# A gated mix of a state-space layer and a feed-forward layer: three parameter loads placed behind the w1 loads, and their four small products later on TensorE

## The chip, the cores and the metric

One Trainium2 chip, one core of it. The metric is the time of one execution on the device in microseconds (us). TensorE (PE) multiplies into PSUM, which has 8 banks here; VectorE (DVE), ScalarE (ACT) and GpSimd (POOL) compute on SBUF; SyncE (SP) only issues transfers (DMAs). All engines run their own instructions in order and wait for each other by semaphores.

## The reference, cut to what matters

```python
x = A_x                                        # [1, 2048, 448], bf16
g = sigmoid((x * gate_w).sum(-1, keepdims=True))
Lam = Lambda_re + 1j * Lambda_im               # 448 channels
dt = exp(log_dt)
Lam_bar = exp(dt * Lam)
B_bar = ((Lam_bar - 1.0) / Lam)[:, None] * (B_re + 1j * B_im)
Bu = einsum("bld,pd->blp", x + 0j, B_bar)
h_t = Lam_bar * h_{t-1} + Bu_t                 # over 2048 tokens
a = 2.0 * einsum("blp,dp->bld", h, C_re + 1j * C_im).real + x * Dskip
b = silu(x @ w1) @ w2                          # w1 [448, 1792], w2 [1792, 448]
out = g * a + (1 - g) * b
```

## The kernel before, in words

The 2048 tokens are taken in four chunks of 512. For each chunk TensorE computes x times w1 (14 blocks of 128 columns, called F tiles) and x times B (7 blocks, B tiles; real and imaginary rows of 448 channels are packed in 7 slots). ScalarE applies silu while it copies the F tiles from PSUM to `aT` (L634); the B tiles go to `UG` (by VectorE at L640 for the first chunk, by ScalarE at L642 after). The complex recurrence is turned into a real one: `UG` is rotated by the angles of each token (tables `COS` and `SIN`, products L704 on VectorE), a scan runs along the tokens with a real factor `rc` (L736), and the result is rotated back into `H`. The readout multiplies `H` by prepared rows of C (`CP`, L795), the second feed-forward product multiplies `aT` by w2 (L774), ScalarE scales that to `fe` (L780), GpSimd's DMA adds it to what the gate made of x (L782), and VectorE joins the two and SP stores (L798, L801).

**Tables and parameters.** `parameters()` (L529 to L589) needs the three vectors log_dt, Lambda_re and Lambda_im, each loaded as one row of 448 values into `prm`. VectorE copies 64 of their columns behind the others (L538), four products on TensorE with a 3x3 identity turn the rows into columns (L536), VectorE copies them out (`pc`, L540), GpSimd takes e to the power of log_dt (L543), and VectorE makes the angle `ph` of each channel (L544) and its fraction of a turn (L524, L527). From `ph` VectorE and ScalarE build `SIN` and `COS` (L555 to L566), the factors of the recurrence and, at last, the scales of C.

**Loads.** w1 is loaded in column groups, `w1cuts = [0, 256, 512, 1024, 1792]`. A group's rows come in two loads, rows 0 to 383 and rows 320 to 447 (w1 has 448 rows, and the second load repeats 64 of them); group 0 is split further. `load()` (L387, DMA issue at L390) gives each load the next number as its priority, so SP's queue follows the order of the calls at L401 to L441: half of x, half of group 0, the three parameters, groups 1 and 2 (two loads each), B (four loads), group 3, the gate and skip vectors, the second chunk of x, w2, C, the rest of x. The other half of x and of group 0 goes on ScalarE's queue.

**TensorE's order** is written out by hand. `x_products` (L647) takes tiles in pairs; each pair accumulates in two banks, in two halves: `half(k, 0)` has 8 matmuls and `half(k, 1)` 6, after which the pair is evicted. The order is half(0, 0), then for each k half(k+1, 0) and half(k, 1). A dictionary `fill` puts other work between: key -1 right behind half(0, 0), key k behind step k, key (k, 0) behind the first of step k's two halves, which is half(k+1, 0) for most. The first two pairs of F tiles need w1's groups 0 and 1, the third and fourth group 2.

**The other engines' order** comes from a planner (`Plan.order`, L104): it simulates the engines with a cost for each operation and takes, at each point, the ready operation of the lowest priority number. What it finds is fixed: each engine then runs that list in order. So a change in one place can reorder VectorE, ScalarE and GpSimd everywhere.

Of the kernel before, what the change touches and what calls it, by code (L numbers as in the profile page):

```python
# [276 lines left out]
def bass_gated_mix__ssm_conv_s5__dense_activation_silu__prompt_kernel(nc, A_x, A_Lambda_re, A_Lambda_im, A_B_re, A_B_im, A_C_re, A_C_im,  # L277
               A_log_dt, A_Dskip, B_x, B_w1, B_w2, gate_w, out):
    with ExitStack() as ctx:
# [3 lines left out]
        def sb(name, shape, dtype):  # L283
            return E(nc.sbuf_tensor(name, list(shape), dtype))
# [38 lines left out]
        prm = sb("prm", [3, 512], BF16)  # L323
# [30 lines left out]
        def sem():  # L354
            _s[0] += 1
            return E(nc.semaphore(name=f"d{_s[0]}"))
# [30 lines left out]
        def load(q, dst, src, name, nbytes, prio=None, after=()):  # L387
            nl[0] += 1
            prio = nl[0] if prio is None else prio
            P.add(q, lambda e: e.dma_start(dst, src), list(after), name.split(), 0.6 if q == "pool" else 0.5, prio, sem(), nbytes, tag="ld " + name)  # L390
# [3 lines left out]
        def load_w1(q, k, a, b):  # L394

            cols = slice(w1cuts[k], w1cuts[k + 1])
            src = B_w1[320:448, cols] if a == 3 else B_w1[128 * a:128 * b, cols].rearrange("(b p) f -> p b f", p=128)
            load(q, w1s[:, 3, cols] if a == 3 else w1s[:, a:b, cols], src, " ".join(f"w1_{k}_{i}" for i in range(a, b)),
                 256 * (b - a) * (cols.stop - cols.start))
# [3 lines left out]
        load_w1("sp", 0, 0, 2)  # L403
        load_w1("act", 0, 2, 3)
        load_w1("act", 0, 3, 4)
        for k, v in enumerate((A_log_dt, A_Lambda_re, A_Lambda_im)):
            load("sp", prm[k:k + 1, 0:448], v.rearrange("(o n) -> o n", o=1), f"prm{k}", 896)
        for k in range(1, len(w1cuts) - 2):
            load_w1("sp", k, 0, 3)
            load_w1("sp", k, 3, 4)  # L410
        Bnat = H[3][:, :, 0:D_MOD]
        load("sp", Bnat[:, 0:3, :], A_B_re[0:384, :].rearrange("(b p) d -> p b d", p=128), "H3_0 H3_1 H3_2", 384 * 896)
        load("sp", Bnat[0:64, 3, :], A_B_re[384:448, :], "H3_3", 64 * 896)
# [84 lines left out]
        def x_transposes(tc, who):  # L498

            tk = Ps(2)  # L500

            def mm(pe):
                for q in range(4):
                    for b in range(4):
                        o = (q * 4 + b) * 64
                        for h in range(2):
                            p = slice(64 * h, 64 * h + 64)
                            r = pe.transpose(bk(tk, h).bitcast(BF16)[:, o:o + 64],  # L508
                                             xnat[p, 4 * tc + b, XCOL[q]:XCOL[q] + 128], ident[p, p])
                return r  # L510
            PE(mm, [f"xn{tc}", "ident"], [tk], 16 * 0.035, f"xT{tc}")
            for h in range(2):
                src = lambda h=h: bk(tk, h).bitcast(BF16).rearrange("p (q b n) -> p q b n", q=4, b=4)
                dst = xT[:, :, tc * CH:(tc + 1) * CH].rearrange("p q (b h n) -> p q b h n", h=2, n=64)[:, :, :, h, :]
                if who[h] == "d":
                    DVE(lambda e, src=src, dst=dst: e.tensor_copy(dst, src()), [tk], [f"xT{tc}_{h}"], 0.69, 2.2, "xTe")
                else:
                    ACT(lambda e, src=src, dst=dst: e.activation(dst, src(), AF.Copy), [tk], [f"xT{tc}_{h}"], act_cost(1024), 2.2, "xTe")
# [74 lines left out]
        def b_transposes(s0, s1, who):  # L593

            tk = Ps(2)
            n = s1 - s0

            def mm(pe):
                for i in range(4):
                    for q in range(n):  # L600
                        o = (i * n + q) * 64
                        for h in range(2):
                            p = slice(64 * h, 64 * h + 64)
                            r = pe.transpose(bk(tk, h).bitcast(BF16)[:, o:o + 64], Bnat[p, s0 + q, XCOL[i]:XCOL[i] + 128], ident[p, p])  # L604
                return r
            PE(mm, [f"H3_{s}" for s in range(s0, s1)] + ["H3_3i"] * (s0 <= 3 < s1) + ["ident"], [tk], n * 4 * 0.0285, "BT")
            for h in range(2):
                src = lambda h=h: bk(tk, h).bitcast(BF16)[:, 0:256 * n].rearrange("p (i s c) -> p i s c", i=4, s=n)
                dst = BT[:, :, :].rearrange("p i (s h c) -> p i s h c", h=2, c=64)[:, :, s0:s1, h, :]
                names = [f"BT{s}_{h}" for s in range(s0, s1)]  # L610
                if who[h] == "d":
                    DVE(lambda e, src=src, dst=dst: e.tensor_copy(dst, src()), [tk], names, 0.15 + n * 0.136, 2, "BTe")
                else:
                    ACT(lambda e, src=src, dst=dst: e.activation(dst, src(), AF.Copy), [tk], names, act_cost(256 * n), 2, "BTe")
# [82 lines left out]
        def F(tc, a=0, b=NFB):  # L697
            return [("F", tc, k) for k in range(a, b)]

        def B(tc):  # L700
            return [("B", tc, k) for k in ((3, 0, 4, 1, 5, 2, 6) if tc else (0, 1, 2, 3, 4, 5, 6))]
# [131 lines left out]
        def gates(tc):  # L833
            xnn = ["xn00", "xn01"] if tc == 0 else [f"xn{tc}"]
            b4 = slice(4 * tc, 4 * tc + 4)
            tt(xg[:, :, :], xnat[:, b4, :], gwb[:, None, :].to_broadcast([128, 4, D_MOD]), ALU.mult,
               xnn + ["gwb"] + (["Gf0"] if tc else []), ["xg"], 1792, 19, "xg")
            tt(xnat[:, b4, :], xnat[:, b4, :], dkb[:, None, :].to_broadcast([128, 4, D_MOD]), ALU.mult,
               xnn + ["dkb"] + (["Gf0"] if tc else []), [f"xd{tc}"] + xnn, 1792, 19, "xd")
            for b in range(4):  # L840
                tb = 4 * tc + b
                ACT(lambda e, tb=tb, b=b: e.activation(junk[:, :], xg[:, b, :], AF.Copy, accum_out=zl[:, tb:tb + 1]),  # L842
                    ["xg"], ["junk", f"zl{tc}"], act_cost(448, 1), 8, "z")
            ACT(lambda e: e.activation(th[:, b4], zl[:, b4], AF.Tanh, scale=0.5), [f"zl{tc}", "tbl"], [f"th{tc}"], 0.25, 8)
            ACT(lambda e: e.activation(g1[:, b4], th[:, b4], AF.Copy, scale=-0.5, bias=0.5), [f"th{tc}"], [f"g1_{tc}"], 0.2, 3, "g")
            ACT(lambda e: e.activation(g[:, b4], th[:, b4], AF.Copy, scale=0.5, bias=0.5), [f"th{tc}"], [f"g_{tc}"], 0.2, 3, "g")
            for b in range(4):
                tb = 4 * tc + b
                ACT(lambda e, tb=tb: e.activation(Tb[:, tb, :], xnat[:, tb, :], AF.Copy, scale=g[:, tb:tb + 1]),  # L849
                    [f"xd{tc}", f"g_{tc}"], [f"Tb{tb}"], act_cost(448, 1), 8, "xd*g")  # L850

        def xt(tc, who):
            return [lambda: x_transposes(tc, who)]
# [7 lines left out]
        def C(*tbs):  # L861
            return [lambda tb=tb: readout(tb) for tb in tbs]

        turn_b = [lambda: b_transposes(0, 2, "da"), lambda: b_transposes(2, 4, "da"), lambda: b_transposes(4, 7, "da")]
        NH = 8
        K = NH // 2
        x_products(F(0, 0, NH) + B(0) + F(0, NH) + B(1),
                   {-1: [parameters], (K - 2, 0): turn_b[:1], K - 2: turn_b[1:2], K - 1: turn_b[2:], 7: xt(1, "da") + [lambda: lanes(0)]}, [K - 2])
        gates(0)
        gates(1)  # L870
        lanes(1)
# [47 lines left out]
```

## Time and profile before

| | |
|---|---|
| median of 3 runs | 142.11 us (142.05 to 142.25) |
| the profiled execution | 141.99 us |
| its span, first to last instruction | 140.2 us |
| granted TensorE clock | 1.000 |
| TensorE busy | 135.7 us, 97% of the span |
| VectorE busy | 122.3 us, 87% |
| ScalarE busy | 89.7 us, 64% |
| GpSimd busy | 38.9 us, 28% |

The busy rows tell how full an engine is, not what sets the end. That is read from the chain that ended last, which follows the work back from the last instruction to whatever released it. Two of its kinds of piece are no computing: "SPq" is SP issuing transfers, one after the other, and "DMA" is a transfer that something waited for. In the timelines each row has a start, a duration, the engine, the line and the tile written; `x4` behind it means four instructions in a row; a bracket at the end gives the idle time of that engine just before, and what ended it. In the table by stretches each engine has its busy time and its count of instructions, and the last three columns are the granted clock, the DMA engines' busy share and their GB/s.

### The profile page before, as it was taken

The page shows a single profiled execution, that of the slowest core. Times are in us where ns is not written, and L with a number is a line of the kernel's source. Part 1 is how long each engine was busy: PE and PEld are TensorE (multiplying, and loading weights), DVE is VectorE, ACT ScalarE, POOL GpSimd, SP SyncE. Part 2 cuts the span into 40 slices and gives each one's busy share as a digit, 9 for nine tenths or more (in the row PEclk, how much of TensorE's full clock was granted, in tenths as well). Part 3 has the DMA queues.
Part 4 walks back from the last instruction along what each step waited for, and adds up shares of the span by engine and source line. Part 5 has one row for each costly group of instructions (what it writes and reads, how often), then busy time and mean ns, then how long its engine had stood idle before and what let it go on. Part 6 is the DMA issues. An engine that isn't in the chain of part 4 may idle for free.

```text
span 140.2 us, 2999 instructions
## 1 busy us (share of the span) xinstructions
PE 135.7 (97%) x1201; PEld 67.7 (48%) x1201; DVE 122.3 (87%) x179; ACT 89.7 (64%) x157; POOL 38.9 (28%) x72
## 2 busy tenths in 40 slices
PE   7979999999999999999999999999999999999992
PEld 2536554455544544455554544444455555555561
DVE  0486999999999999999999999999999999992053
ACT  3239978999999996713961886799930298011300
POOL 7340030202436500139550003732000223122220
PEclk9999999999999999999999999999999999999999
DMA  4899999610466730109985000946002304323332
GB/s 159 248 356 263 370 297 209 194 42 0 72 108 107 115 40 0 37 0 137 148 145 136 0 5 0 151 92 101 0 0 101 65 0 70 72 91 54 47 91 73
DMA packets 17956, 14.71 MB, mean 105 GB/s; under 512 B 2835, under 2 KB 17814, under 8 KB 17942
## 3 DMA queue, kind: packets, MB, share of 16 engines
q0 software_dynamic: 6064, 5.51, 24.8%
q1 hardware_dynamic: 11318, 8.65, 21.0%
q10 hardware_dynamic: 560, 0.36, 0.8%
q8 instruction: 9, 0.15, 0.4%
q14 instruction: 5, 0.04, 0.1%
HBM read 7.17 MB, written 1.84 MB: 64 GB/s over the span
## 4 chain that ended last, share of the span: by engine, by line
PE 92%; DMA 3%; SPq 2%; issue 0%; DVE 0%
PE ps L663 44%; PE ps L774 30%; PE ps L795 15%; DMA w1s<-in_B_w_dram 3%; SPq L390 2%; PE ps L508 1%; PE ps L814 1%; PE ps L604 1%; DVE ot L798 0%
## 5 line engine op out<-in xcount | busy, mean ns | idle before, releaser
L663 PE MATMUL ps<-xT,w1s 64*128 64x512 bf16 x392 | 48.2, 376 | 0.9 <-DMA w1s<-in_B_w_dram 0.9
L774 PE MATMUL ps<-w2s,aT 128*128 128x448 bf16 x224 | 43.2, 353 | 0.0
L634 ACT ACTIVATE aT<-ps 128x1024 bf16<-128x1024 f32 (+1 forms) x30 | 28.5, 966 | 11.2 <-PE ps L663 11.1
L774 PEld LDWEIGHTS ps<-w2s,aT 128*128 128x128 bf16 x224 | 21.7, 98 | 20.4 <-issue 0.4
L663 PEld LDWEIGHTS ps<-xT,w1s 64*128 64x128 bf16 x392 | 19.8, 94 | 22.8 <-DMA w1s<-in_B_w_dram 1.4
L663 PE MATMUL ps<-xT,BT 64*128 64x512 bf16 x196 | 25.8, 376 | 0.0
L782 POOL DMA_DIRECT2D xnat<-fe x16 | 14.2, 890 | 41.5 <-ACT fe L780 35.7
L780 ACT ACTIVATE fe<-ps,g 128x448 bf16<-128x448 f32 x16 | 10.1, 631 | 19.9 <-PE ps L774 19.9
L390 POOL DMA_DIRECT2D UG<-Gf x27 | 14.8, 555 | 26.1 <-DVE Gf L736 25.8
L798 DVE SCALAR_TENSOR_TENSOR ot<-ps,g,xnat 128x448 bf16<-128x448 f32 (+2 forms) x18 | 10.8, 626 | 8.0 <-issue 6.6
L736 DVE TENSOR_TENSOR_SCAN Gf<-rc,gin,H 128x512 f32<-128x512 f32 x14 | 17.0, 1268 | 0.0
L795 PE MATMUL ps<-CP,H 128*128 128x448 bf16 (+2 forms) x98 | 16.4, 326 | 0.0
L663 PEld LDWEIGHTS ps<-xT,BT 64*128 64x128 bf16 x196 | 11.1, 94 | 10.9 <-issue 0.2
L704 DVE TENSOR_TENSOR H<-UG,COS 128x3584 bf16<-128x3584 bf16 (+4 forms) x10 | 12.7, 1270 | 0.0
L795 PEld LDWEIGHTS ps<-CP,H 128*128 128x128 bf16 x98 | 8.9, 98 | 7.5 <-DVE PO L704 0.4
L642 ACT ACTIVATE UG<-ps 128x1024 bf16<-128x1024 f32 (+1 forms) x12 | 10.9, 919 | 1.3 <-PE ps L663 1.3
L390 POOL DMA_DIRECT2D UG<-UG x8 | 4.5, 564 | 24.3 <-ACT UG L642 13.6
L842 ACT ACTIVATE junk<-xg 128x448 bf16<-128x448 bf16 x16 | 9.3, 579 | 3.0 <-DVE xg L704 2.9
L849 ACT ACTIVATE xnat<-xnat,g 128x448 bf16<-128x448 bf16 x16 | 9.9, 659 | 0.3
L704 DVE TENSOR_TENSOR PI<-UG,SIN 128x512 bf16<-128x512 bf16 (+2 forms) x13 | 9.2, 728 | 0.0
L704 DVE TENSOR_TENSOR PO<-UG,SIN 128x1536 bf16<-128x1536 bf16 (+1 forms) x8 | 8.7, 1085 | 0.3 <-DMA UG<-Gf 0.2
L736 DVE TENSOR_TENSOR_SCAN Gf<-rc,gin,H2C 128x512 f32<-128x512 f32 x7 | 8.6, 1270 | 0.0
(102 smaller groups left out, 126.5 us busy)
## 6 DMA issues: line engine op xcount, KB each, us to landing
UG<-Gf POOLq DMA_DIRECT2D x21, 128.0 KB, 2.3
xnat<-fe POOLq DMA_DIRECT2D x16, 112.0 KB, 2.6
out_dram<-ot SPq DMA_DIRECT2D x15, 112.0 KB, 1.7
w2s<-in_B_w_dram SPq DMA_DIRECT2D x1, 1568.0 KB, 11.5
xnat<-in_A_x_dram SPq DMA_DIRECT2D x3, 448.0 KB, 6.6
w1s<-in_B_w_dram SPq DMA_DIRECT2D x1, 576.0 KB, 5.4
UG<-UG POOLq DMA_DIRECT2D x8, 64.0 KB, 2.0
H2C<-in_A_C_re_dram SPq DMA_DIRECT2D x2, 196.0 KB
```

The costliest lines, as they stand in the source:

```text
L390: P.add(q, lambda e: e.dma_start(dst, src), list(after), name.split(), 0.6 if q == "pool" else 0.5, prio, sem(), nbytes, tag="ld " + name)
L634: ACT(lambda e, src=src, dst=dst: e.activation(dst, src(), AF.Silu), [tk, "tbl"], [f"aT{tc % 2}_{m}" for m in names], act_cost(512 * n), 2 ...
L642: ACT(lambda e, src=src, dst=dst: e.activation(dst, src(), AF.Copy), [tk], [f"{un}{m}" for m in names], act_cost(512 * n), 5, "U")
L663: r = pe.matmul(bk(toks[k], b), weights(tile, p0, p0 + 64, i), xT[p0:p0 + 64, i, tc * CH:(tc + 1) * CH], start=(h == 0 and n == 0), stop=( ...
L704: DVE(lambda e: e.tensor_tensor(o, a, b, op), r, w, dve_cost(n, 2), prio, tag)
L736: DVE(lambda e, s=s, b=b, init=init: e.tensor_tensor_scan(Gf[:, s, :], rc[:, b:b + 1].to_broadcast([128, CH]), A[:, s, :], init, ALU.mult, ...
L774: r = pe.matmul(bk(tk)[:, 0:D_MOD], aT[tc % 2][:, fb, o:o + 128], w2s[:, fb, :], start=(fb == 0), stop=(fb == NFB - 1))
L780: ACT(lambda e: e.activation(f[:, :], bk(tk)[:, 0:D_MOD], AF.Copy, scale=g1[:, tb:tb + 1]), [tk, f"g1_{tc}"], [fn], act_cost(448, 1), 7, "fe")
L782: P.add("pool", lambda e: e.dma_start(Tb[:, tb, :], f[:, :], accum_op=ALU.add), [fn, f"Tb{tb}"], [f"Tb{tb}"], 0.94, 2, sem(), 115000, tag= ...
L795: r = pe.matmul(bk(tk)[:, 0:b - a], H[tc][:, s, o:o + 128], CP[:, s, a:b], start=(s == 0), stop=(s == NSLOT - 1))
L798: DVE(lambda e, tk=tk, a=a, b=b: e.scalar_tensor_tensor(ot[tb % NOT][:, a:b], bk(tk)[:, 0:b - a], g[:, tb:tb + 1], Tb[:, tb, a:b], ALU.mul ...
L849: ACT(lambda e, tb=tb: e.activation(Tb[:, tb, :], xnat[:, tb, :], AF.Copy, scale=g[:, tb:tb + 1]), [f"xd{tc}", f"g_{tc}"], [f"Tb{tb}"], ac ...
```

## The change

```diff
         load_w1("sp", 0, 0, 2)
         load_w1("act", 0, 2, 3)
         load_w1("act", 0, 3, 4)
-        for k, v in enumerate((A_log_dt, A_Lambda_re, A_Lambda_im)):
-            load("sp", prm[k:k + 1, 0:448], v.rearrange("(o n) -> o n", o=1), f"prm{k}", 896)
         for k in range(1, len(w1cuts) - 2):
             load_w1("sp", k, 0, 3)
             load_w1("sp", k, 3, 4)
+        for k, v in enumerate((A_log_dt, A_Lambda_re, A_Lambda_im)):
+            load("sp", prm[k:k + 1, 0:448], v.rearrange("(o n) -> o n", o=1), f"prm{k}", 896)
         Bnat = H[3][:, :, 0:D_MOD]
...
         x_products(F(0, 0, NH) + B(0) + F(0, NH) + B(1),
-                   {-1: [parameters], (K - 2, 0): turn_b[:1], K - 2: turn_b[1:2], K - 1: turn_b[2:], 7: xt(1, "da") + [lambda: lanes(0)]}, [K - 2])
+                   {(1, 0): [parameters], (K - 2, 0): turn_b[:1], K - 2: turn_b[1:2], K - 1: turn_b[2:], 7: xt(1, "da") + [lambda: lanes(0)]}, [K - 2])
```

On SP's queue the three parameter loads move behind the four loads of w1's groups 1 and 2 and ahead of B's. On TensorE the four small products move from behind half(0, 0) to behind half(2, 0): ahead of them stand now 30 matmuls of the F tiles instead of 8, behind them half(1, 1), half(3, 0) and the first transposes of B. Nothing is added or taken away; the number of transfers, matmuls and other operations is the same.

As the planner now meets the parameters later, it orders the other engines anew. On VectorE the evictions of B's transposes (L612) and of the first B tiles (L640) stand among the operations on the angles (L524 to L562), the first L612 right behind the first `ph` (L544) and its rounding (L524). On ScalarE the small sines of L574 to L576 and the tables of L560 and L563 come behind all three evictions of B's transposes (L614); the last two pairs of tables stand between silu evictions. The first chunk's gate sums (L842, four of them) stood between evictions of F and B tiles and follow each other now behind the last eviction of the second chunk's B tiles (L642); of the second chunk's four, one instead of four comes before the fourth `fe` (L780).

## The prediction

> **What bounds the kernel now.** I read the page's first two parts, then the chain that ended last, then what TensorE waited for, then the timeline of the first 12 us, and last DMA traffic by stretches. The page:
>
> ```profile
> PE 135.7 (97%) x1201; PEld 67.7 (48%) x1201; DVE 122.3 (87%) x179; ACT 89.7 (64%) x157; POOL 38.9 (28%) x72
> PE ps L663 44%; PE ps L774 30%; PE ps L795 15%; DMA w1s<-in_B_w_dram 3%; SPq L390 2%; PE ps L508 1%; PE ps L814 1%; PE ps L604 1%; DVE ot L798 0%
> ```
>
> TensorE holds the end: 92% of the chain is its work, and the only pieces that are not work of an engine are SP's issuing (2%) and one w1 transfer (3%). The granted clock is 1.00 in every slice. The chain in order of time shows where these pieces lie:
>
> ```profile
> 2.39 0.25 SPq L390
> ...
> 2.68 0.39 SPq L390
> ...
> 4.12 4.39 DMA w1s<-in_B_w_dram
> 8.51 0.14 issue
> 8.64 2.55 PE ps L663 x22
> ```
>
> So the start is a queue: SP issues x, w1, the three parameter loads, then w1's next four; the last of those four (columns 512 to 1023, rows 320 to 447) is issued at 4.12 and lands at 8.51; TensorE starts on it at 8.64 and from there hardly rests until 137.46. A microsecond won or lost before 8.64 moves the end by as much, until another wait takes over. Among TensorE's waits this is the only one after the start-up:
>
> ```profile
> PE ps L663 <- DMA w1s<-in_B_w_dram: 0.9, 1, 0.9
> PE ps L463 <- PEq L904: 0.8, 1, 0.8
> ```
>
> The timelines of SP and TensorE give the parts that change:
>
> ```profile
> 1.72 0.35 SPq L390 DMA_DIRECT2D prm<-in_A_log_dt_dram  x1
> 2.11 0.23 SPq L390 DMA_DIRECT2D prm<-in_A_Lambda_re_dram  x1
> 2.39 0.25 SPq L390 DMA_DIRECT2D prm<-in_A_Lambda_im_dram  x1
> 2.68 1.92 SPq L390 DMA_DIRECT2D w1s<-in_B_w_dram  x4
> ...
> 5.83 0.25 PE L536 MATMUL ps<-ident,prm 3*128 3x3 bf16 x4
> 6.01 1.68 PE L663 MATMUL ps<-xT,w1s 64*128 64x512 bf16 x14
> 8.64 2.55 PE L663 MATMUL ps<-xT,w1s 64*128 64x512 bf16 x22 [0.95 <-DMA w1s<-in_B_w_dram]
> ```
>
> and the traffic by stretches (the last two columns are DMA busy share and GB/s):
>
> ```profile
> 2.10:3.90 1.80, 1.80 (x17) 0.62 (x17) 0.00 (x0) 1.28 (x1) 1.61 (x9) 1.00 1.08 344
> 3.90:4.20 0.30, 0.30 (x20) 0.30 (x16) 0.14 (x1) 0.14 (x1) 0.25 (x3) 1.00 0.80 204
> 4.80:5.10 0.30, 0.30 (x8) 0.15 (x4) 0.30 (x2) 0.19 (x1) 0.00 (x0) 1.00 0.89 197
> 5.10:5.70 0.60, 0.60 (x8) 0.16 (x4) 0.26 (x2) 0.00 (x0) 0.00 (x0) 1.00 0.60 83
> 5.70:6.30 0.60, 0.60 (x10) 0.33 (x10) 0.17 (x1) 0.00 (x0) 0.00 (x0) 1.00 0.77 244
> ```
>
> The engines ran at 344 GB/s while x and the first w1 columns moved, then fell to 83 around 5.4, before the third w1 group came up to speed. The reader should see a hole in the traffic just ahead of the transfer that TensorE waits for.
>
> **Part 1, the w1 loads go ahead of the parameters on SP.** The three parameter issues take from 1.72 to 2.68, 0.96 us. The four w1 issues move from 2.68-4.60 to 1.72-3.64; the parameter issues then stand at about 3.69, 4.08 and 4.36; the B loads stay at 4.65, as nothing is added. So the deciding load is issued 0.96 earlier. How much earlier does it land? At most 0.96, if landing follows issue. At least 0, if the engines were already short of rate. The hole decides: against 344 GB/s the missing traffic is (344-204)x0.3 + (344-197)x0.3 + (344-83)x0.6 + (344-244)x0.6 = 303 kB, or 0.88 us at 344. By the change the third group is issued at 2.69 instead of 3.65, while the earlier bytes still move, so its slow start lies beside them. Not all of the hole is won (4.20 to 4.80 moved only 294 GB/s in 512-byte rows, so that rate limits there). I take 0.75: landing at 7.76, TensorE at 7.89.
>
> The second group (issue to landing 2.7 and 2.6 us, at 5.72) also comes sooner, but that only lets TensorE start its 14 products at about 5.7 instead of 6.01 and wait from about 7.2: no gain of its own.
>
> **Part 2, the four small products move on TensorE.** Before, they stood at 5.83, ahead of the wait, so their 0.18 us (5.83 to 6.01, the next weight load) was hidden by it. Now they stand behind the third pair's first half, after the wait, on the path. Price: 0.18 by that row, up to 0.42 if the idle time that the weight load row puts before them (0.42, "issue") recurs. I take 0.20, as the row that times them is the nearest.
>
> **Part 3, the wait that is added.** TensorE is in order, so behind these products wait all its others. They need the loads and one VectorE copy (L538: 0.17; in the trace it ends at 5.49 and the product's weights load at 5.83; with 0.10 to wake it, 0.61 from landing to product). TensorE gets there 8 products after 7.89, at 2.55/22 each, 0.93: 8.82. So the parameters may land up to 8.2 for nothing. Before, the last was issued at 2.39 and read at 5.32, at most 2.93 later: by that row 7.3 now. The load behind them, B's first (issued 4.65, 336 KB), took 5.0: by that row 9.36. They are 0.9 KB each and queue behind the third w1 group, so I expect them with it, at 7.5 to 8.0: no wait.
>
> **Part 4, everything that the parameters feed is later.** From the product at 5.83 to ph on VectorE at 7.46 is 1.63 us (1.05 of it GpSimd's power); now 8.82 + 1.63 = 10.45, 3.0 later. VectorE did 3.0 us of this work between 7.46 and 10.42, then waited 1.05 for the first B transposes; that gap takes in some, so later VectorE work slips by 1.9 to 3.0. Who waits for that? The last recurrence: its H is done at 126.89 on VectorE (124.80 plus 2.09), and TensorE's last readout starts at 131.95. That cover is 5.06, or 4.5 if TensorE comes 0.55 sooner. Enough; without it every microsecond over would count in full. The evictions of B and of its first products, which TensorE does need at once, are placed between the angle instructions in the changed order, so they don't queue behind the whole table. The first of them, L612, stands behind the first ph and its rounding: 10.45 + 0.16 + 0.17, 10.8 or so, when its transposes (11.02 plus 0.41 before, 0.55 less now) end at 10.9. Nothing.
>
> ScalarE: sine and cosine slip too, and with them the first gates and the evictions of the w2 products at 32 to 42. It is nearly full there. In the changed order three fewer of the gate sums (L842, 0.70 us apart where they follow each other) come before the fourth of those evictions, 2.1 us, against the slip of up to 3.0: at worst 0.9 late, less the gaps (0.66 at 19.48, 0.37 at 22.14). I take 0, bound 0.9.
>
> **Sum.** -0.75 + 0.20 = -0.55 us on the profiled execution, which took 141.99 (span 140.2 and 1.8 around it). That execution is 0.12 below the median of 142.11; I shift the median: 142.11 - 0.55 = 141.56, say 141.6. Its own bounds: -0.96 + 0.18 = -0.78, 141.3; with a gain of 0.5, -0.3, 141.8.
>
> **Rivals.**
>
> *The engines are full anyway (24%).* If the slow stretch from 5.1 to 6.3 belongs to this transfer (its rows, its place in memory) and not to when it was issued, it only moves and the group lands 0 to 0.3 sooner. Then the products' 0.2 eats it: -0.1 to +0.2, 142.0 to 142.3. For it: SP had issued the group's first load by 4.08, a microsecond before the hole at 5.1. Against it: x, issued at 0.73 to idle engines, needed about 1.1 us to its first bytes, too, and the busy share in the hole is 0.60 and not 1. The Trainium skill's page DMA: Bandwidth & Descriptors (section Issuing engines are not separate DMA queues) states that time saved in issuing is usually small beside the transfer itself; by that rule the sum would be near +0.2. The trace speaks against it here only through the hole.
>
> *TensorE stands at the small products (14%, slower).* The place: L536, third pair. The price: if the parameters land like B's first load, at 9.36, the product runs at 9.97 instead of 8.82, 1.15 late: -0.55 + 1.15 = +0.6, 142.7. It costs from a landing at 8.2 and makes the kernel slower from 9.0. For it: three loads of 0.9 KB behind 768 KB of w1 on one queue. Against it: their transfers are tiny, and before they were there within 2.93 us behind 352 KB on SP's queue. The same page (Queues, rings and completion order) states that each engine takes its ring's descriptors in order and that a load's semaphore does not wait for other engines' rings; by that the three would wait only for one engine's share of w1, at or before w1's own landing.
>
> *ScalarE or VectorE comes late at 30 to 42 (8%).* The fourth w2 eviction is late for the banks of the next w1 products: up to +0.9 on -0.55, 141.9 to 142.5.
>
> **How the numbers follow.** Forecast (141.2 to 141.9): 54%. The measurement of this kernel can tell about 0.2%, 0.28 us, from no change. Faster by more than that needs a gain of 0.5 or more at the landing and no new wait: 55%. Within 0.2%: 26%, the first rival and part of the third. Slower: 19%, the second rival and the bad ends of the other two. The range, 141.2 to 142.5, takes in the forecast, the first rival and most of the third, and leaves out the second's worst.
>
> **What would show it.** In the changed profile: SP's parameter issues at 3.7 to 4.6; the hole at 5.1 to 6.3 gone or shallower; TensorE's wait on w1 ending near 7.9; the products L536 near 8.8 without a wait ahead of them; VectorE's ph near 10.4; VectorE's idle time before the last readouts down from 6.6 to about 4.5, with H still ahead of TensorE. Wrong if the wait on w1 still ends after 8.4, if L536 waits more than 0.3, or if TensorE shows a new wait between 30 and 43.

## The result, and the profile after

The changed kernel took 141.47 us (median of 6 executions, 141.25 to 141.68) beside 142.18 for the kernel before on the same chip (6 executions): a ratio of 0.9955, 95% interval 0.9933 to 0.9976. The profiled execution took 141.25 us, its span is 139.5, and the granted clock 0.998; before these were 141.99 and 140.2. The kernel was measured twice more, 12 executions each beside 23 of the kernel before: 141.62 against 142.01, ratio 0.9983 (0.9962 to 1.0004), and 141.74 against 142.19, ratio 0.9976 (0.9956 to 0.9996). These figures leave out three of the 24 executions, at 144.0 to 144.4, of which no profile was taken (and one each of e1 and e6 and two of e5, below), while none of the kernel before's 46 took more than 142.8. So the change is worth 0.2 to 0.5%, and the second measurement by itself cannot be told from no change; the forecast was 0.4%.

The page of the changed kernel, engines and chain:

```profile
PE 135.9 (97%) x1201; PEld 67.0 (48%) x1201; DVE 122.0 (87%) x179; ACT 90.3 (65%) x157; POOL 39.2 (28%) x72
PE 97%; DVE 0%; issue 0%
PE ps L663 46%; PE ps L774 31%; PE ps L795 15%; PE ps L463 2%; PE ps L508 1%; PE ps L478 1%; PE ps L814 1%; PE ps L604 1%; DVE ot L798 0%; PE ps L675 0%; PE ps L464 0%; PE ps L536 0%
```

The w1 transfer (3%) and SP's issuing (2%) are gone from the chain, and nothing but TensorE is left: it is followed through the x transposes down to the first instructions. The four small products now stand on it. The chain in order of time (start, duration, what):

```profile
5.00 3.82 PE ps L663 x30
8.82 0.18 PE ps L536 x4
9.00 1.62 PE ps L663 x14
10.62 0.23 PE ps L604 x16
...
20.10 8.20 PE ps L663 x76
```

One piece of 30 matmuls runs from 5.00 into the products, where before 22 of them had ended by 7.7 and TensorE then stood until 8.64. At the pace of before (2.55 us for 22) 30 would take 3.48, so some 0.3 us of waiting is left inside the 3.82. SP's timeline shows the new order of issue:

```profile
1.20 2.51 SPq L390 DMA_DIRECT2D w1s<-in_B_w_dram  x5
3.75 0.33 SPq L390 DMA_DIRECT2D prm<-in_A_log_dt_dram  x1
4.12 0.23 SPq L390 DMA_DIRECT2D prm<-in_A_Lambda_re_dram  x1
4.39 0.25 SPq L390 DMA_DIRECT2D prm<-in_A_Lambda_im_dram  x1
```

and the traffic by the same stretches as before (last two columns: DMA busy share, GB/s):

```profile
3.90:4.20 0.30, 0.30 (x16) 0.23 (x12) 0.14 (x1) 0.14 (x1) 0.25 (x3) 1.00 1.24 280
...
4.80:5.10 0.30, 0.30 (x6) 0.16 (x4) 0.30 (x3) 0.27 (x1) 0.00 (x0) 1.00 1.18 328
5.10:5.70 0.60, 0.60 (x4) 0.00 (x0) 0.22 (x2) 0.00 (x0) 0.00 (x0) 1.00 1.08 364
5.70:6.30 0.60, 0.60 (x8) 0.20 (x8) 0.00 (x0) 0.00 (x0) 0.00 (x0) 1.00 1.09 377
```

The hole is filled: 364 GB/s from 5.10 to 5.70 where 83 moved before. In the list of DMA issues (KB each, us from issue to landing) the load that TensorE had waited for, issued at 3.22, is this row:

```profile
w1s<-in_B_w_dram SPq DMA_DIRECT2D x1, 128.0 KB, 4.4
```

It took 4.4 us, as before (4.39 from 4.12), so with an issue 0.90 earlier it landed 0.89 earlier, at 7.62. TensorE's weight loads show what it did with that (in brackets the idle time before the row, and what ended it):

```profile
4.86 0.16 PEld L663 LDWEIGHTS ps<-xT,w1s 64*128 64x128 bf16 x4
5.73 0.14 PEld L663 LDWEIGHTS ps<-xT,w1s 64*128 64x128 bf16 x4 [0.70 <-DVE xT L486]
6.24 1.22 PEld L663 LDWEIGHTS ps<-xT,w1s 64*128 64x128 bf16 x14 [0.37 <-DMA w1s<-in_B_w_dram]
7.73 0.60 PEld L663 LDWEIGHTS ps<-xT,w1s 64*128 64x128 bf16 x8 [0.27 <-issue]
8.75 0.16 PEld L536 LDWEIGHTS ps<-ident,prm 3*128 3x128 bf16 x4 [0.42 <-issue]
8.93 1.19 PEld L663 LDWEIGHTS ps<-xT,w1s 64*128 64x128 bf16 x14
```

The third group's weights (half(2, 0)) start at 7.73, 0.88 before their 8.61 of the kernel before. The row names no DMA any more, yet it stands 0.1 us behind the landing at 7.62, as the 8.61 stood behind 8.51; but the matmuls now run on without a pause, and the first of half(2, 0) starts at 7.78. The rows ahead came later: the second part of half(0, 0) at 5.73 instead of 5.24, half(1, 0) at 6.24 instead of 6.01. The label of the first is misleading: L486, which it names, had ended at 5.32. What it needed as well is group 0's last load, on ScalarE's queue, issued at 1.77 and landed 3.9 us later, at 5.6. The waits left are now those on groups 0 and 1, and TensorE reaches group 2 just as it lands.

**The sum, from the two traces.** The first matmul of half(2, 0) starts 0.86 earlier (7.78 instead of 8.64). From there to the first transposes of B (L604) it is 2.84 us (7.78 to 10.62) instead of 2.56 (8.64 to 11.20): +0.28 for the products. The piece of 76 matmuls at 20.10 is 8.20 long; before it was 8.33: -0.13. Together -0.71; the spans differ by 0.7.

### The profile page after: what moved, and what is told of

Its sections match the earlier page's. It is cut to its first block, busy times and chain, and to the rows that moved or that the text cites. A ratio compares the mean times of both kernels' runs of the same rounds, so it can differ in the third digit from the quotient of the medians.

```text
span 139.5 us, 3000 instructions
## 1 busy us (share of the span) xinstructions
PE 135.9 (97%) x1201; PEld 67.0 (48%) x1201; DVE 122.0 (87%) x179; ACT 90.3 (65%) x157; POOL 39.2 (28%) x72
## 4 chain that ended last, share of the span: by engine, by line
PE 97%; DVE 0%; issue 0%
PE ps L663 46%; PE ps L774 31%; PE ps L795 15%; PE ps L463 2%; PE ps L508 1%; PE ps L478 1%; PE ps L814 1%; PE ps L604 1%; DVE ot L798 0%; PE ps L675 0%; PE ps L464 0%; PE ps L536 0%
## 5 line engine op out<-in xcount | busy, mean ns | idle before, releaser
L663 PE MATMUL ps<-xT,w1s 64*128 64x512 bf16 x392 | 48.5, 378 | 0.0
L663 PEld LDWEIGHTS ps<-xT,w1s 64*128 64x128 bf16 x392 | 19.7, 94 | 22.3 <-DVE xT L486 0.7
L663 PE MATMUL ps<-xT,BT 64*128 64x512 bf16 x196 | 25.8, 376 | 0.0
L780 ACT ACTIVATE fe<-ps,g 128x448 bf16<-128x448 f32 x16 | 10.1, 632 | 21.1 <-PE ps L774 21.0
L663 PEld LDWEIGHTS ps<-xT,BT 64*128 64x128 bf16 x196 | 10.8, 94 | 11.1 <-DVE Gf L562 0.2
L798 DVE SCALAR_TENSOR_TENSOR ot<-ps,g,xnat 128x448 bf16<-128x448 f32 (+2 forms) x18 | 10.8, 622 | 6.0 <-issue 4.6
L642 ACT ACTIVATE UG<-ps 128x1024 bf16<-128x1024 f32 (+1 forms) x12 | 10.7, 923 | 1.4 <-PE ps L663 1.4
L842 ACT ACTIVATE junk<-xg 128x448 bf16<-128x448 bf16 x16 | 9.2, 574 | 2.1 <-DVE xg L704 2.0
L849 ACT ACTIVATE xnat<-xnat,g 128x448 bf16<-128x448 bf16 x16 | 9.8, 671 | 0.2
```

The costliest lines, as they stand in the source:

```text
L663: r = pe.matmul(bk(toks[k], b), weights(tile, p0, p0 + 64, i), xT[p0:p0 + 64, i, tc * CH:(tc + 1) * CH], start=(h == 0 and n == 0), stop=( ...
L780: ACT(lambda e: e.activation(f[:, :], bk(tk)[:, 0:D_MOD], AF.Copy, scale=g1[:, tb:tb + 1]), [tk, f"g1_{tc}"], [fn], act_cost(448, 1), 7, "fe")
L798: DVE(lambda e, tk=tk, a=a, b=b: e.scalar_tensor_tensor(ot[tb % NOT][:, a:b], bk(tk)[:, 0:b - a], g[:, tb:tb + 1], Tb[:, tb, a:b], ALU.mul ...
```

## The experiments

Each kernel ran beside the kernel before on the same chip; "changed" is the kernel of the document.

**e1_loads_only: the loads moved, the products left behind half(0, 0).** Against the changed kernel:

```diff
-                   {(1, 0): [parameters], (K - 2, 0): turn_b[:1], ...
+                   {-1: [parameters], (K - 2, 0): turn_b[:1], ...
```

> The loads are moved as in the change, the four small products stay behind half(0, 0). If the parameters really land with or after w1's third group, as the changed kernel's trace shows (VectorE read them at 8.16), TensorE stands at L536 until about 8.7 with 14 products less behind it than the kernel before had at 8.64: 1.7 to 1.9 us slower than before, about 144.0. Rival: transfers of 0.9 KB land early wherever they stand in the queue, as they did before (read at 5.32): then nothing waits and it is the changed kernel less 0.18, 141.3.

Ratio 1.0118 (1.0040 to 1.0195). Its four executions lie apart, at 143.29, 143.33, 145.38 and 145.66; what follows is read from the one of 143.33, whose span is 141.5. A piece of its chain:

```profile
4.39 3.24 DMA prm<-in_A_Lambda_im_dram
```

and of TensorE's timeline:

```profile
8.14 0.23 PE L536 MATMUL ps<-ident,prm 3*128 3x3 bf16 x4 [1.67 <-DVE prm L538]
```

The parameters land at 7.63; the products, now asked for at 6.5, stand 1.67 us, and all 36 matmuls behind them run without a pause, as group 2 is there by then. The traffic from 5.10 to 5.70 is 313 GB/s. So the order of the loads alone fills the hole, and it costs more than it wins unless the products move too. Against the first profile of the kernel before the span grew by 1.3, less than the theory's 1.7 to 1.9, as the products ran at 8.14 and not at 8.7.

**e2_products_only: the products moved, the loads left.** Against the kernel before:

```diff
-                   {-1: [parameters], (K - 2, 0): turn_b[:1], ...
+                   {(1, 0): [parameters], (K - 2, 0): turn_b[:1], ...
```

> The small products move as in the change, the loads stay as before. If the loads' place alone gives the gain and the products cost their own time behind the wait, it is 0.2 slower than before: 142.3 to 142.4, the wait for w1's third group ends near 8.6 as before, and L536 takes 0.18 behind it. Rival: a part of the gain came from the products' absence ahead of the wait: 141.7 to 142.0.

142.6 us, ratio 1.0020 (1.0003 to 1.0038). Its chain:

```profile
4.14 4.45 DMA w1s<-in_B_w_dram
8.72 1.04 PE ps L663 x8
9.94 1.62 PE ps L663 x14
...
21.05 8.20 PE ps L663 x76
```

The wait is back (landing at 8.59), and the hole too (125 GB/s from 5.10 to 5.70). From half(2, 0) at 8.72 to the first L604 at 11.56 it is 2.84 us, 0.28 more than before. That prices the products without any change in the loads. The piece of 76 matmuls is 8.20 here and in every profile with the products behind half(2, 0), and 8.32 or 8.33 in e1, e4 and a second profile of the kernel before, which have them behind half(0, 0): these 0.13 us come with the place of the products, by the order that the planner then finds. The traces point to a copy of VectorE: the first product behind the second chunk's transposes of x (L508) needs a bank that a copy L640 empties. In the kernel before that copy stands behind L527 and starts at 19.36, and the product comes 0.60 us behind the first transpose (20.64 after 20.03); in the changed kernel it starts at 18.43, and the product comes 0.47 behind (19.94 after 19.47). That this copy makes the difference was not tried by itself.

**e3_delayed_no_small: the changed order, but SP issues groups 1 and 2 later.** SP's loads from the sixth on wait for a small GpSimd instruction (the iota of `pidx`, which is done at 2.33), so groups 1 and 2 are issued from 2.36 instead of 1.71, with no small load ahead of them. Against the changed kernel:

```diff
+            if q == "sp" and nl[0] > 5:
+                after = list(after) + ["pidx"]
...
+        POOL(lambda e: e.iota(pidx[:, :], pattern=[[1, 1]], base=0, channel_multiplier=1), [], ["pidx"], 0.1, 2)
...
-        POOL(lambda e: e.iota(pidx[:, :], pattern=[[1, 1]], base=0, channel_multiplier=1), [], ["pidx"], 0.1, 2)
```

> The changed kernel, but SP waits for a small operation of GpSimd (done at about 2.33) before it issues w1's second and third groups, and no small load is ahead of them. If the hole in the traffic comes from late issuing, it is partly back at 5.1 to 5.9, the third group is issued near 3.4 instead of 2.7 and lands near 8.2, and the time is 0.4 to 0.6 above the changed kernel: 141.9 to 142.1. Rival: the three small transfers themselves broke the stream; then there is no hole, the third group lands by 7.9, and the time is 141.5 to 141.7.

141.69 us, ratio 0.9957 (0.9943 to 0.9972). Its chain:

```profile
3.77 4.42 DMA w1s<-in_B_w_dram
...
8.33 1.04 PE ps L665 x8
```

and two rows of its traffic:

```profile
5.10:5.70 0.60, 0.60 (x8) 0.11 (x4) 0.30 (x2) 0.06 (x1) 0.00 (x0) 1.00 0.84 217
5.70:6.30 0.60, 0.54 (x6) 0.14 (x4) 0.00 (x0) 0.00 (x0) 0.00 (x0) 1.00 0.92 328
```

(L665 is L663 of the other kernels.) The last load of group 2 again takes 4.4 us from its issue, now to 8.19; the hole is partly back, between the 83 before and the 364 after. So a later issue brings a part of the hole back. A share of it may still belong to the three small loads as such; late issue and small loads were not tried apart. This trace went as the theory said, the time did not: it was 0.2 to 0.4 lower than expected. The repeat, e8 below, has the same issue and another landing.

**e4_params_on_gpsimd: the parameters on GpSimd's own queue, products behind half(0, 0).** Against e1:

```diff
-            load("sp", prm[k:k + 1, 0:448], v.rearrange("(o n) -> o n", o=1), f"prm{k}", 896)
+            load("pool", prm[k:k + 1, 0:448], v.rearrange("(o n) -> o n", o=1), f"prm{k}", 896, 0.5)
```

> The w1 loads come early as in the change, but the parameters are loaded by GpSimd's queue and their products stay behind half(0, 0). If the parameters land by 5.6, L536 stands in TensorE's wait for w1's first two groups and costs nothing: 0.1 to 0.2 below the changed kernel, 141.3, and VectorE's angles start near 7.5 again. Rival: GpSimd's loads land later than 6.1, TensorE stands at L536 and every bit is paid: landing at 7.1 gives about 142.3.

144.57 us, ratio 1.0157 (1.0138 to 1.0175). The theory, that another queue brings them in time, fell. Its chain:

```profile
2.92 4.69 DMA prm<-in_A_Lambda_im_dram
8.36 5.43 PE ps L663 x36
```

and its table by stretches (the granted clock is the third column from the end):

```profile
6.30:8.40 2.10, 0.89 (x10) 0.44 (x12) 0.17 (x2) 0.00 (x0) 0.00 (x0) 0.86 1.09 340
8.40:11.20 2.80, 2.80 (x14) 0.94 (x14) 1.79 (x10) 0.00 (x0) 2.27 (x3) 0.50 1.05 342
```

Issued 1.5 us sooner than in e1, the last 0.9 KB landed at 7.61, where e1's had landed at 7.63. And the 36 matmuls take 5.43 us where e1 took 3.99, with a granted clock of 0.50 from 8.40 to 11.20: these 1.4 us account for the 1.3 that e4 loses against e1 in span (142.8 against 141.5).

**c1_changed_again and e5_groups_respread.** The first is the changed kernel once more. In e5 SP's queue has the rows 0 to 383 of groups 0, 1 and 2 and group 2's last rows, and ScalarE's the last rows of groups 0 and 1, so that group 0 comes sooner. Against the changed kernel:

```diff
-        load_w1("sp", 0, 0, 2)
-        load_w1("act", 0, 2, 3)
+        load_w1("sp", 0, 0, 3)
         load_w1("act", 0, 3, 4)
+        load_w1("sp", 1, 0, 3)
+        load_w1("act", 1, 3, 4)
+        load_w1("sp", 2, 0, 3)
+        load_w1("sp", 2, 3, 4)
...
-        for k in range(1, len(w1cuts) - 2):
-            load_w1("sp", k, 0, 3)
-            load_w1("sp", k, 3, 4)
```

> The changed kernel itself, unaltered, beside the others on one chip. 0.4% to 0.6% below the kernel before; in its profile TensorE's weights for half(0, 0)'s second part come near 5.7, for half(1, 0) near 6.2, for half(2, 0) near 7.7 without a wait, if the first execution was no accident. Rival: those two early waits were an accident of that execution and lie 0.3 to 0.5 earlier here, with the wait for w1's third group back at half(2, 0) until 7.7.

> The changed kernel with w1's first two groups spread otherwise over the two queues: SP takes rows 0 to 383 of groups 0, 1 and 2 and the last rows of group 2, ScalarE's queue takes the last rows of groups 0 and 1. If w1's group 0 is late in the changed kernel because its second load on ScalarE's queue (issued at 1.72) shares the DMA engines with the early group 1, it lands near 5.0 here, TensorE comes to half(2, 0) near 7.4 instead of 7.7, and the time is 0.2 to 0.4 below the changed kernel. Rival: all bytes up to group 2 must pass anyway and the order among them changes nothing: within 0.1 of the changed kernel.

c1: 141.62, ratio 0.9983 (0.9962 to 1.0004). Its profile repeats the first one: half(0, 0)'s second part at 5.71, half(1, 0) at 6.21, half(2, 0) at 7.73. e5: 141.48, ratio 0.9972 (0.9943 to 1.0000); three of its twelve executions took 143.1 to 143.2. In its profile half(1, 0) starts at 6.03, half(2, 0) at 7.58 and L536 at 8.64, so 0.1 to 0.2 earlier than in c1; the times do not tell the two apart. Inconclusive on time.

**e6_params_after_step3, e7_params_after_step2: the products later still.** They ask how much of the cover that the prediction named is there. Against the changed kernel, e6 (e7 has `[parameters]` behind `turn_b[1:2]`):

```diff
-                   {(1, 0): [parameters], (K - 2, 0): turn_b[:1], K - 2: turn_b[1:2], K - 1: turn_b[2:], ...
+                   {(K - 2, 0): turn_b[:1], K - 2: turn_b[1:2], K - 1: turn_b[2:] + [parameters], ...
```

> The changed kernel, with the parameters' products still later, behind step 3 and B's last transposes, about 4.5 later on TensorE. If the last recurrence is the only cover that counts, as the prediction had it (4.6 us of VectorE idle time ahead of the last readouts are left), the time stays within 0.3 of the changed kernel, 141.4 to 141.8. Rival: ScalarE, whose sines then stand ahead of its evictions, makes TensorE wait between 20 and 32 for banks: 1.5 to 3 us more, 143.0 to 144.5, with the waits at the transposes of C (L814) and the first w2 products (L774).

> As the run before, but behind step 2, about 2.9 later on TensorE than in the changed kernel. Last recurrence as the only cover: 141.4 to 141.7. ScalarE as the next bound: already here a part of the loss, 142.0 to 144.5, as its order puts the sines ahead of the first evictions to UG (L642).

144.51 us, ratio 1.0171 (1.0147 to 1.0196), and 144.60, ratio 1.0183 (1.0162 to 1.0205). The products run at 13.78 in e6 and at 11.75 in e7, 5.0 and 3.0 later than in the changed kernel. What TensorE waited for in e6 (us in total, times, longest):

```profile
PE ps L814 <- ACT UG L642: 1.1, 1, 1.1
...
PE ps L774 <- ACT UG L642: 0.5, 1, 0.5
PE ps L663 <- ACT tr L574: 0.5, 1, 0.5
```

and three pieces of its chain:

```profile
17.72 0.68 ACT junk L842 x2
19.05 2.35 ACT xnat L849 x4
...
30.27 1.40 ACT UG L642 x2
```

The planner now puts the first chunk's gate sums (L842) and products (L849) ahead; the small sines (L574) stand at 22.68 instead of 14.54, and the evictions of the second chunk's B tiles (L642) begin at 30.16 instead of 26.32. TensorE stands until the banks that they empty are free. In e7 it waits 1.6 us for the same evictions (L642), and 0.8 for VectorE's copy of B's transposes (L612). VectorE is still idle for 4.0 us before the last readouts in e6 and 4.2 in e7, and the last H is done about 2.5 us before TensorE reads it. So what decides first when the parameters come later is the order of ScalarE near 30 us, and in e7 of VectorE too, as the third rival had it, and not the last recurrence.

**c2_changed_third, e8_delayed_again, b2_before_again.** The changed kernel a third time, e3 a second time, and a second profile of the kernel before, all beside each other.

> The changed kernel once more, unaltered. If its gain differs from execution to execution because all of x and the first three w1 groups now compete for the same traffic at the start (in four profiles with this order of loads half(2, 0) began at 7.73, 7.73, 8.22 and 8.13), the executions spread over about 1 us and the median lies 0.2% to 0.5% below the kernel before. Rival: the second measurement's smaller gain was a matter of that call: the ratio is 0.9955 again, within 0.1%.

> The kernel whose second and third w1 groups wait for GpSimd's small operation, again, now beside the changed kernel. If early issue counts to the end, it is 0.2 to 0.5 above the changed kernel (half(2, 0) at 8.3 against 7.7). Rival: with group 0 left undisturbed it is as fast, within 0.1, and spreads less.

> The kernel before, for a second profile of it: the hole between 5.1 and 6.3, the wait for w1's third group until 8.5 to 8.7, the third group's last load 4.3 to 4.5 after its issue. Rival: the hole was an accident of the first profile, then the wait ends before 8.2.

c2: 141.74, ratio 0.9976 (0.9956 to 0.9996), the executions counted from 141.35 to 142.54. e8: 141.48, ratio 0.9957 (0.9939 to 0.9974), all twelve from 141.37 to 141.77. The kernel with the later issue is at least as fast as the changed one, and its time varies a third as much; that it is faster is not shown, as the intervals overlap. c2's profile shows what varies:

```profile
1.77 4.39 DMA w1s<-in_B_w_dram
6.30 3.03 PE ps L663 x26
9.51 1.62 PE ps L663 x14
```

Here the load that ends the last wait is group 0's last one, on ScalarE's queue: 4.39 us, landing at 6.16, half a microsecond later than in the first profile, and half(2, 0) starts at 8.26 instead of 7.73. But group 2's last load was no earlier: issued at 3.23 in c2, it landed at 8.15, half a microsecond later too. So TensorE again came to half(2, 0) just as it landed, and the later start cannot be put on group 0 alone. The rows of this load in c2 and in e8, where it was issued at 3.77 (KB, us to landing):

```profile
w1s<-in_B_w_dram SPq DMA_DIRECT2D x1, 128.0 KB, 4.9
w1s<-in_B_w_dram SPq DMA_DIRECT2D x1, 128.0 KB, 3.8
```

In e8 it landed at 7.6, as early as in the first profile of the changed kernel, though issued 0.55 later and with 245 GB/s in the hole; in e3, the same kernel with the same issue, it landed at 8.19. So the landing did not follow the issue there. In e3 and e8, where SP issues groups 1 and 2 some 0.6 later, the second part of half(0, 0) starts at 5.45 and 5.40 instead of 6.27. b2 gives the other side of the comparison: the kernel before waited until 9.10 in this execution (8.61 in the first), with 143 GB/s in the hole. Over the profiles taken, half(2, 0) starts at 8.61, 8.69 and 9.10 with the old order of loads, and at 7.73, 7.73, 8.26, 8.13 and 8.22 with the new one (c2, e7 and e6 the last three); in e5, e3 and e8 it is 7.58, 8.29 and 7.7.

## Why the prediction was right, step by step

**What bounds the kernel.** Right: a microsecond won before 8.64 came back at the end. The last readouts start 0.73 earlier (131.22 instead of 131.95), and the span is 0.7 shorter.

**Part 1, landing 0.75 earlier (0 to 0.96).** The direction was right, the size low: issued 0.90 earlier, the load landed 0.89 earlier in the first pair of profiles, and TensorE's first product on it came 0.86 earlier. The deduction from the hole, that some of it could not be won, did not hold in this pair. That the landing follows the issue is not shown beyond it: from issue to landing the load took 4.4 us in the changed kernel's first two profiles and 4.9 in the third, 4.4 in e3 and 3.8 in e8. What all profiles show is the order of the loads: group 2 landed at 8.51, 8.59 and 9.00 behind the three small loads, and at 7.45 to 8.28 in the ten profiles without them ahead of it on its queue. Whether their issuing time or the small loads themselves held it up stays open.

What the step missed is that the earlier loads pay: it took group 2 alone for the limit and said that group 1 comes sooner. Group 1 was issued about 1 us earlier and landed at 5.9 and 6.1 instead of 5.3 and 5.7, and group 0's last load took 3.9 us instead of 3.1. That took nothing in the first profile, since group 2 landed at 7.62 anyway, but it left nothing to be won by a still earlier landing. In c2 all three groups landed about half a microsecond later than in the first profile; why is open. The three measurements give -0.71, -0.40 and -0.45 us in their medians, around the forecast's -0.55; as the landing alone differs by half a microsecond between executions of one kernel, that it lies among them is in part luck.

The Trainium skill's page DMA: Bandwidth & Descriptors states (Queues, rings and completion order) that each DMA engine takes turns between the queues that have work for it. The trace of the first pair agrees: the load on ScalarE's queue had been issued at the same time in both kernels and landed 0.7 later when more stood on SP's queue. But in b2, with the old order, it took 3.8 us too, so a part of that is the execution's.

**Part 2, the products at 0.20 (0.18 to 0.42).** Mis-sized: 0.28 in the first profile, and 0.28 in e2, which has the old loads. The 0.42 of idle weight loading ahead of them, which the prediction gave as the other end, recurs in all nine profiles with the products behind half(0, 0) or half(2, 0) where they wait for nothing (8.75 above). It lies beside a running matmul in part, and so the price is between the two rows. The nearest row was not a price, as before it lay beside a wait.

**Part 3, no wait.** Right that there was none. VectorE's timeline of the changed kernel:

```profile
8.16 0.17 DVE L538 COPY prm<-prm 3x64 bf16<-3x64 bf16 x1 [2.84 <-DMA prm<-in_A_Lambda_im_dram]
...
10.38 0.16 DVE L544 SCALAR_TENSOR_TENSOR ph<-dtc,pc 128x4 f32<-128x4 f32 x1 [0.88 <-POOL dtc L543]
10.58 0.17 DVE L524 TENSOR_SCALAR phk<-ph 128x4 f32<-128x4 f32 x1
10.89 0.42 DVE L612 COPY BT<-ps 128x512 bf16<-128x512 bf16 x1
```

The parameters were read at 8.16. In e1 they were read at 7.82, 0.19 us behind their landing at 7.63, so here they landed near 7.97: inside the 7.5 to 8.0, and 0.2 before the step's limit of 8.2. The products ran at 8.76, 0.06 before the 8.82 forecast. In c1 the read came earlier:

```profile
7.49 0.17 DVE L538 COPY prm<-prm 3x64 bf16<-3x64 bf16 x1 [2.30 <-DMA prm<-in_A_Lambda_im_dram]
```

There the landing was near 7.3, and in c2 (read at 8.21) near 8.0. The second rival was thus 0.2 us from beginning to cost in the first profile, and 0.9 in c1. e1 shows what the wait costs where it stands on the path: 1.67 us.

The prediction drew from the Trainium skill's DMA: Bandwidth & Descriptors (Queues, rings and completion order) that the three would come at or before w1's own landing, as a load waits only for its own engines' share. The traces are divided: the three came about 0.3 us before group 2's last load in c1 (7.3 against 7.63), 0.3 behind it in the first profile (7.97 against 7.62), and 0.2 behind it in e1 (7.63 against 7.45).

**Part 4, the chain behind the parameters.** `ph` at 10.38 (10.45 forecast), the first L612 at 10.89 (10.8). VectorE's idle time before the last readouts, from the waits:

```profile
DVE ot L798 <- issue: 4.6, 1, 4.6
```

4.5 was forecast. It is made up otherwise than the text had it: the last H is done at 128.16, 1.27 later than before and not 1.9 to 3.0, and TensorE comes 0.73 sooner. The cover that the prediction counted, from that H to TensorE's last readout, shrank from 5.06 to 3.06. TensorE shows no wait between 30 and 43, so ScalarE cost its 0. The cover named, the last recurrence, was not the one that ends first: e7 and e6, with the products 3.0 and 5.0 us later, lose some 2.9 us against the changed kernel, over half of it in waits for ScalarE, while about 2.5 us of that cover are left.

**Sum.** Forecast -0.75 + 0.20 = -0.55; traces -0.86 + 0.28 - 0.13 = -0.71. Two errors of about 0.1 cancel, and the -0.13 of the planner's new order was not foreseen at all.

**Rivals.** The engines were not full: in the changed kernel's three profiles the group landed at 7.62, 7.63 and 8.15, where the kernel before has 8.51 and 9.00, and the hole was filled (364, 358 and 376 GB/s from 5.10 to 5.70, where before had 83 and 143). The Trainium skill's DMA: Bandwidth & Descriptors (Issuing engines are not separate DMA queues) states that the time saved in issuing is usually small beside the transfer, from which the prediction drew a sum near +0.2. That did not come out: 0.90 us of earlier issue went with 0.89 at the landing in the first pair, beside 4.4 from issue to landing. e8, where the load came as early with a later issue, forbids making a rule of it. TensorE at the small products: not here, with 0.2 us to spare, and the whole loss of e1. ScalarE or VectorE late: not here, and over half of the loss of e6 and e7.

## What to carry to other kernels

Tiny loads ahead of the awaited one on the same queue can cost as much as their issuing times at the head of the critical path: 0.9 us in the first pair of profiles. A hole in the traffic ahead of the awaited transfer was the sign; whether the issuing or the small loads themselves make it was not separated. Look also at the loads already under way: here the waits on the first two groups grew until TensorE reached the third just as it landed, so a still earlier landing would have won nothing. One pair of profiles does not size such a gain, as the same load of the same kernel landed at 7.6 in two executions and at 8.15 in a third. And moving what waits for the small loads is half of the change: either half alone made this kernel slower.

## What the runs showed of the hardware

- The last load of 0.9 KB took about 2.9 us (c1), 3.2 (e1) and 3.6 (the first profile of the changed kernel) from issue to landing behind w1 on SP's queue, and 4.7 on GpSimd's queue beside that traffic (e4). A queue of its own did not help it there.
- The same 128 KB load of w1 took 3.8 to 5.1 us from issue to landing over the 13 profiles, and 4.4 and 3.8 in two executions of the same kernel (e3, e8).
- In e4 TensorE was idle for 1.21 and 0.72 us of the time from 5.58 to 8.12; its granted clock was 0.86 from 6.30 to 8.40 and 0.50 from 8.40 to 11.20 (in finer stretches, 0.50 from 7.8 to 11.2), and the matmuls there cost 1.44 us more than e1's. In e1 one wait of 1.67 us left the clock at 1.00 in the profiled execution; its execution of 145.38 has a mean granted clock of 0.988, as all four of e4 have. The Trainium skill's page TensorE: Matmul & The Clock Gate (Part 1: The HAM clock gate) states that the clock is halved after an idle window of about 3.4 us, which runs freely and isn't reset by the kernel. The half rate agrees with the 0.50 here, and 7.8 to 11.2 is as long as such a window; the idle times were shorter than that, so whether that window was the cause stays open.
